# One tile for both kinds of a batch's spectrum rows, one send for its last rows, and Pool's half stores moved to the sync queue

## Chip, cores, metric

One core of one Trainium2 chip. The metric is the device time of one execution in microseconds. The time of a run is about 1.8 us longer than the span of its profile.

In the views PE is the matmul engine and PEld its loading of weights; DVE, ACT and POOL are the vector, scalar and GpSimd engines; SP is the sync engine. DMAs are issued by an engine to a queue of its own (SPq is sync's) and carried out by 16 DMA engines. A store goes from the chip's inner memory to the output; a half store is one of 64 rows (128 KB); a send is a small DMA between two tiles on the chip. A DMA has landed when its data is in place.

## The reference, cut to what matters

```python
x = windowed_attention(q, k, v)            # 8 batches x 576 x 512
X = rfft(x, axis=1)                        # first 64 modes kept
Y[:, :64] = complex_matmul_per_mode(X, w_r, w_i)
u = x + irfft(Y, n=576)
return u + relu(u @ w_ch)                  # 8 x 576 x 512, float32
```

## The kernel before, where the change touches it

The kernel streams all mode weights, then ends in a tail (from about 392 us) that turns the spectra back. For each batch two tables of 128 spectrum rows are needed as the moving operand: `Yb` (the spectrum) and `yw` (the spectrum times w_ch). The last eight rows of each come from the last four modes; for batches 2 to 7 the kernel gathers them in `yl` and sends them by DMA to their place, partitions 120 to 127.

```python
def pair_tile(what, b):                    # one tile per kind and pair of batches
    p = b // 2
    if (what, p) not in Yp:
        Yp[what, p] = wmid.tile([128, 2, DM], FP32R, ...)
    return Yp[what, p][:, b % 2, :]
...
yl = yp.tile([128, 2, DM], FP32R, name="yl")
def send(i, b):                            # 8 rows x 2 KB
    r0 = 2 * R + RL * (b - 2)
    nc.gpsimd.dma_start(out=pair_tile(("yw", "Yb")[i], b)[128 - RL:], in_=yl[r0:r0 + RL, i])
...
def finish(n):                             # one output piece of 128 rows x 512
    b, t = seq[n]
    add(n, "Yb", True)                     # PE
    if t % 2 == 0:
        ots[0] = op.tile([128, 2, DM], FP32, name="ot")     # 7 buffers
    ...
    nc.vector.tensor_tensor(out=ot[:, j], in0=ps, in1=x_sb[:, b, t, :], op=ALU.add)
    if t == NT - 1:                        # 64 rows of batch b, 64 of b + 1
        for i, queue in enumerate((nc.sync, nc.gpsimd)):
            queue.dma_start(out=out[b + i, 128 * t:, :], in_=ot[64 * i:64 * i + 64, 0])
    ...
    elif j:                                # two pieces, 128 rows x 4 KB
        nc.sync.dma_start(out=..., in_=ot)
...
for n in range(NT):
    rectify(n)                             # PE add of yw, then ReLU on ACT
    if n == 2:
        nc.scalar.copy(out=yl[0:NR, 0], in_=psw[0:NR])
for b in range(2, B):
    for i in range(2):
        send(i, b)
for n in range(NQ):                        # 36 pieces
    finish(n)
    ...                                    # rectify and lay three ahead
```

The softmax here doesn't subtract the row's maximum and nothing guards it: scores larger than these inputs give would overflow.

## Time and profile before

| | before |
|---|---|
| time, median (range) | 429.94 us (429.93 to 430.3) |
| span of the profile, in a run of 431.18 us | 429.4 us |
| DVE's last output piece ends | 421.33 us |
| last store issued, landed | 423.82, 428.37 us |

The profiled run was 1.2 us slower than the median. Part 3 of its page lists each DMA queue with its packets, MB and share of the 16 engines:

```profile
q0 software_dynamic: 25920, 82.52, 96.4%
q1 hardware_dynamic: 2768, 8.78, 5.5%
```

Queue 0 is Pool's: all loads of weights and of q, k and v, and in the tail the sends and four half stores. Queue 1 is sync's: all other stores but one. The tail shares its 16 DMA engines between both.

### The profile page before, as it was taken

How to read it: one execution, taken by the hardware profiler on the slowest of the kernel's cores; microseconds unless marked ns; L12 is line 12 of the kernel's file. 1: busy time of each engine (PE TensorE's matmuls, PEld its weight loads, DVE VectorE, ACT ScalarE, POOL GpSimd, SP SyncE). 2: the span in 40 equal slices, each digit the busy share in tenths (PEclk: the TensorE clock that was granted, in tenths of full speed). 3: DMA queues.
4: the chain of work that ended last, by engine and by line, in shares of the span. 5: the costliest groups of instructions: out<-in, count | busy, mean ns of one | idle time of the engine just before them, and what ended most of it. 6: DMA issues, size and time to landing. Idle time of an engine off the chain costs nothing.

```text
span 429.4 us, 11626 instructions
## 1 busy us (share of the span) xinstructions
PE 322.8 (75%) x5186; PEld 230.2 (54%) x5186; DVE 176.6 (41%) x372; ACT 164.5 (38%) x290; POOL 97.9 (23%) x187
## 2 busy tenths in 40 slices
PE   6989999999989966323488978876367875598991
PEld 4755765665665665212366756654244543356780
DVE  5566765766673200307233432231022331132892
ACT  3585765866773121001021322222012231122990
POOL 7231231331021322212212212111211122100600
PEclk9999999999995855555587998899557785589996
DMA  7999999999999999999999999999999999992897
GB/s 140 212 213 211 214 214 213 213 213 212 214 214 214 215 213 260 214 213 213 213 214 214 214 214 212 214 213 214 213 214 213 213 213 214 213 203 43 270 363 266
DMA packets 28882, 92.17 MB, mean 215 GB/s; under 512 B 3136, under 2 KB 3392, under 8 KB 28832
## 3 DMA queue, kind: packets, MB, share of 16 engines
q0 software_dynamic: 25920, 82.52, 96.4%
q1 hardware_dynamic: 2768, 8.78, 5.5%
q8 instruction: 40, 0.66, 0.6%
q10 hardware_dynamic: 144, 0.13, 0.1%
q14 instruction: 10, 0.08, 0.0%
HBM read 162.53 MB, written 9.44 MB: 400 GB/s over the span
## 4 chain that ended last, share of the span: by engine, by line
DMA 47%; PE 32%; issue 9%; DVE 7%; ACT 1%; POOL 1%; DVEq 0%; POOLq 0%
DMA wt<-in_moe_w_i_dram 25%; DMA wt<-in_moe_w_r_dram 21%; PE pso L316 7%; PE pst L218 6%; PE psv L235 3%; DVE x_sb L324 3%; PE pso L856 3%; PE pss L372 3%; PE pss L272 2%; PE psx L338 2%; PE pss L291 2%; DVE vT L59 2%; PE psz L594 1%; PE psy L563 1%; PE psw L706 1%
## 5 line engine op out<-in xcount | busy, mean ns | idle before, releaser
L563 PE MATMUL psy<-XQ,wt 128*128 128x16 bf16 x1616 | 61.1, 191 | 73.1 <-DMA wt<-in_moe_w_i_dram 37.2
L563 PEld LDWEIGHTS <-wt 128*128 128x128 bf16 x1616 | 52.8, 103 | 88.6 <-DMA wt<-in_moe_w_i_dram 43.3
L591 DVE CAST xT<-pxt 128x256 fp32r<-128x256 bf16 (+1 forms) x68 | 26.2, 435 | 60.1 <-PE pxt L584 38.9
L115 POOL DMA_DIRECT2D wt<-in_moe_w_r_dram x54 | 29.0, 537 | 87.7 <-DMA wt<-in_moe_w_r_dram 39.2
L115 POOL DMA_DIRECT2D wt<-in_moe_w_i_dram x52 | 28.1, 540 | 85.6 <-DMA wt<-in_moe_w_i_dram 54.9
L596 ACT CAST Z<-psz 128x512 fp32r<-128x512 f32 x36 | 21.1, 587 | 65.3 <-PE psz L594 64.9
L594 PE MATMUL psz<-wch,xT 128*128 128x512 f32 x144 | 46.1, 464 | 0.0
L297 ACT ACTIVATE et<-pss 128x512 bf16<-128x512 f32 x72 | 39.2, 599 | 13.6 <-PE pss L291 13.6
L316 PE MATMUL pso<-vt,et 128*64 128x65 bf16 (+1 forms) x576 | 34.3, 210 | 4.8 <-DVE x_sb L324 4.7
L316 PEld LDWEIGHTS <-et 128*64 128x64 bf16 (+1 forms) x576 | 24.0, 114 | 17.1 <-issue 9.6
L594 PEld LDWEIGHTS psz<-wch,xT 128*128 128x128 f32 x144 | 29.4, 218 | 6.0 <-ACT Z L596 0.4
L324 DVE TENSOR_TENSOR x_sb<-pso,rcp 128x640 bf16<-128x640 f32 x32 | 26.3, 822 | 0.9
L59 DVE CAST YT<-psy 128x256 fp32r<-128x256 f32 x6 | 2.5, 425 | 51.1 <-PE psy L563 51.1
L879 DVE TENSOR_TENSOR ot<-pso,x_sb 128x512 f32<-128x512 f32 x35 | 22.3, 686 | 1.8 <-PE pso L856 1.5
L59 DVE CAST x_sb<-psj 128x512 bf16<-128x512 f32 x16 | 11.0, 689 | 27.5 <-PE psj L768 27.4
L58 ACT CAST YT<-psy 128x256 fp32r<-128x256 f32 x6 | 2.2, 373 | 52.4 <-DVE YT L59 52.4
L272 PE MATMUL pss<-band,ident_bf 64*64 64x512 bf16 x136 | 20.7, 414 | 1.5 <-ACT et L297 1.5
L59 DVE COPY vT<-pst 128x768 bf16<-128x768 bf16 x16 | 15.3, 958 | 13.0 <-PE pst L218 13.0
L58 ACT CAST x_sb<-psj 128x512 bf16<-128x512 f32 x16 | 9.4, 587 | 27.3 <-PE psj L768 27.3
L861 ACT ACTIVATE pso<-pso 128x512 f32<-128x512 f32 x36 | 19.2, 587 | 0.3 <-PE pso L856 0.2
L291 PE MATMUL pss<-qT,kT 64*64 64x128 bf16 (+1 forms) x640 | 17.3, 221 | 0.4 <-issue 0.4
L58 ACT COPY qT<-pst 128x768 bf16<-128x768 bf16 x16 | 12.9, 815 | 7.8 <-PE pst L218 7.6
(163 smaller groups left out, 518.5 us busy)
## 6 DMA issues: line engine op xcount, KB each, us to landing
wt<-in_moe_w_r_dram POOLq DMA_DIRECT2D x54, 512.0 KB, 19.1
wt<-in_moe_w_i_dram POOLq DMA_DIRECT2D x52, 512.0 KB, 19.1
out_dram<-ot SPq DMA_DIRECT2D x15, 512.0 KB, 5.5
rk<-in_k_dram POOLq DMA_DIRECT2D x8, 576.0 KB, 9.3
rq<-in_q_dram POOLq DMA_DIRECT2D x8, 576.0 KB, 13.3
rv<-in_v_dram POOLq DMA_DIRECT2D x8, 576.0 KB, 11.8
wy<-in_moe_w_r_dram POOLq DMA_DIRECT2D x3, 512.0 KB, 17.9
wy<-in_moe_w_i_dram POOLq DMA_DIRECT2D x3, 512.0 KB, 19.1
```

The lines of the kernel that those rows point to most:

```text
L58: return nc.scalar.copy(out=o, in_=i)
L59: return nc.vector.tensor_copy(out=o, in_=i)
L115: nc.gpsimd.dma_start(out=wt, in_=src[m].rearrange("(p c) e -> p c e", c=NC))
L218: nc.tensor.transpose(out=ps[64 * hh:64 * hh + 64, c, :], in_=src[:, hh, (c0 + c) * D:(c0 + c + 1) * D], identity=ident_bf)
L272: nc.tensor.matmul(out=pss[(2 * w + hh) % 3][64 * half:64 * half + 64, :], lhsT=ident_bf[pp, pp], rhs=view(band[pp], 128 * half, [[0, WIN ...
L291: nc.tensor.matmul(out=pss[(2 * w + hh) % 3][64 * half:64 * half + 64, col:col + nq], lhsT=kTs[b % 2][pp, g, 64 * kb:64 * kb + 64], rhs=qT ...
L297: nc.scalar.activation(out=et[:, hh, :], in_=pss[(2 * w + hh) % 3], func=ACT_F.Exp, scale=EX_SCALE)
L316: nc.tensor.matmul(out=pso[po, hh, (i // 2) * VW:(i // 2) * VW + D + 1], lhsT=et[pk, hh, col:col + 64], rhs=vt[pk, 1 - f % 2, 2 * hh + g / ...
L324: nc.vector.tensor_tensor(out=view(x_sb, b * NT * DM + g * D, [[4 * D, 2], [DM, NT], [1, D]]), in0=view(pso, 0, [[512, 2], [VW, NT], [1, D]]),
L563: nc.tensor.matmul(out=psy[:, m % MG, e, :], lhsT=w[:, c, 128 * e:128 * e + 128], rhs=XQ[:, c, :, 1 - im:3 - im, m], start=(m % MG == im + ...
L591: nc.vector.tensor_copy(out=xT[:, :, w * k:w * k + w], in_=view(psts[k], j, [[128, NC], [n, w]]))
L594: nc.tensor.matmul(out=psz, lhsT=xT[:, c, :], rhs=wch[:, c, :], start=(c == 0), stop=(c == NC - 1))
```

## The change

Its intent: both kinds of a batch's rows lie side by side in one tile, so one DMA with 4 KB runs replaces two with 2 KB runs; and Pool no longer stores.

```diff
+    def batch_tile(b):
+        if b not in Yp:
+            Yp[b] = wmid.tile([128, 2, DM], FP32R, name=f"Y{b}", tag=f"wm{b}")
+        return Yp[b]
     def pair_tile(what, b):
-        p = b // 2
-        ...
-        return Yp[what, p][:, b % 2, :]
+        return batch_tile(b)[:, ("yw", "Yb").index(what), :]
...
-        def send(i, b):
+        def send(b):
             r0 = 2 * R + RL * (b - 2)
-            nc.gpsimd.dma_start(out=pair_tile(("yw", "Yb")[i], b)[128 - RL:], in_=yl[r0:r0 + RL, i])
+            nc.gpsimd.dma_start(out=batch_tile(b)[128 - RL:], in_=yl[r0:r0 + RL])
...
-                for i, queue in enumerate((nc.sync, nc.gpsimd)):
+                for i, queue in enumerate((nc.sync, nc.sync)):
...
         for b in range(2, B):
-            for i in range(2):
-                send(i, b)
+            send(b)
```

More of the change, by code (lines that the diff above doesn't have):

```diff
@@ L688 @@
     Yp = {}
+    def batch_tile(b):
+        if b not in Yp:
+            Yp[b] = wmid.tile([128, 2, DM], FP32R, name=f"Y{b}", tag=f"wm{b}")
+        return Yp[b]
     def pair_tile(what, b):
-        p = b // 2
-        if (what, p) not in Yp:
-            Yp[what, p] = wmid.tile([128, 2, DM], FP32R, name=f"{what}{p}", tag=f"wm{2 * p + (what == 'Yb')}")
-        return Yp[what, p][:, b % 2, :]
+        return batch_tile(b)[:, ("yw", "Yb").index(what), :]
     def parts_of(b, t):
```

## The prediction

> **What bounds the kernel now.** The change touches only the last 8% of the run, so I asked first where that stage begins and what ends it. In the page's busy-share row the DMA engines stand at nine tenths almost throughout; until about 391 us that is the stream of weights, whose code is untouched. I cut the rest into stretches and read the DMA share beside the engines. Columns: stretch, length, busy us of PE, PEld, DVE, ACT and POOL with counts, granted clock, DMA share, GB/s.
>
> ```profile
> 400.00:404.00 4.00, 3.83 (x17) 2.82 (x16) 3.27 (x6) 4.00 (x9) 3.56 (x8) 1.00 0.92 278
> 408.00:412.00 4.00, 4.00 (x19) 3.20 (x18) 3.79 (x7) 4.00 (x9) 0.00 (x0) 1.00 0.98 350
> 412.00:415.00 3.00, 3.00 (x15) 2.43 (x14) 2.70 (x6) 3.00 (x7) 0.53 (x1) 1.00 1.03 415
> 416.00:419.00 3.00, 3.00 (x14) 2.15 (x12) 2.99 (x6) 3.00 (x7) 0.53 (x1) 1.00 0.96 315
> 420.00:421.00 1.00, 0.04 (x1) 0.00 (x0) 1.00 (x4) 0.00 (x0) 0.00 (x0) 1.00 0.82 281
> 426.00:429.40 3.40, 0.00 (x0) 0.00 (x0) 0.00 (x0) 0.00 (x0) 0.00 (x0) 0.50 0.18 66
> ```
>
> From 400 to 421 us PE, ACT, DVE and DMA are all nearly full, so shares alone do not choose. The end does: DVE makes the last output piece at 421.3 us, yet the DMA engines stay full to 426. So the store queue is next (SPq is the sync engine's issue queue; columns are start, length, what).
>
> ```profile
> 420.58 0.75 DVE L876 TENSOR_TENSOR ot<-pso,x_sb 128x256 f32<-128x256 f32 x2
> ...
> 418.86 3.70 SPq L887 DMA_DIRECT2D out_dram<-ot  x3
> 422.66 1.07 SPq L884 DMA_DIRECT2D out_dram<-ot  x1
> 423.82 1.10 SPq L877 DMA_DIRECT2D out_dram<-ot  x1
> ```
>
> The final store is issued at 423.82, about 2.8 us after its data was ready: the queue is behind. Is the sync sequencer slow, or is it held back by full DMA engines? The view of the store lines gives min/median/max ns of an issue, and that of all transfers the us to landing:
>
> ```profile
> L887 SPq DMA_DIRECT2D out_dram<-ot x15: 332/756/2175, 397.9 to 421.8; - x15
> L882 SPq DMA_DIRECT2D out_dram<-ot x4: 515/857/1127, 403.4 to 418.1; - x4
> L882 POOL DMA_DIRECT2D out_dram<-ot x4: 529/538/559, 404.6 to 416.6; - x4
> ```
>
> The same 512 KB store costs 332 ns to issue when the engines are free (the first ones) and up to 2175 ns later. So it waits for room, and I read the tail as bound by the DMA engines' throughput, not by DVE, PE or the sync sequencer. Throughput is uneven: 415 GB/s where only 512 KB sync stores drain, 278 while the last spectrum rows are sent, 315 and 350 where Pool stores are mixed in. That unevenness is what the change can alter. The waits in the tail (engine line <- what ended it: us in total, times, longest) show what else is at stake:
>
> ```profile
> DVE ot L879 <- PE pso L856: 1.5, 7, 0.3
> PEld pso L856 <- DMA yw<-yl: 0.6, 1, 0.6
> POOL Yb L845 <- DMA Yb<-yl: 0.4, 1, 0.4
> ```
>
> Only one compute wait is on the row transfers, 0.6 us at 400.9. DVE never waits for a store, so the seven output buffers suffice, so far.
>
> **What the Trainium skill says.** (1) "DMA: Bandwidth & Descriptors", section "Issuing engines are not separate DMA queues": DMAs started by sync, scalar and gpsimd share 16 engines; several issuers save only sequencer time. The trace agrees: share 0.96 to 1.03 with either mix. (2) Same page, "Why a DMA increments its semaphore by 16 and not by 1": for gpsimd DMAs all 16 engines post a completion, whatever the shape. In the window that holds the sends, the software queue shows
>
> ```profile
> q0 software_dynamic: 269, 0.13, 14.4%
> ```
>
> packets, MB, share of 16 engines over 6.7 us. 0.13 MB in 2 KB pieces is about 64 packets, so some 205 are small ones, over the 192 that twelve sends at 16 would give. Agrees. (3) Same page, "Why small descriptors are slow (HBM only)": SBUF-to-SBUF transfers are said not to suffer the small-descriptor penalty. That speaks against a big gain from 4 KB runs; no view of this kernel separates it. (4) "SBUF — State Buffer", "Door 1: The DMA port swizzle": 64 partitions reach only half the ports (196 against 328 GB/s at 1 MiB). The trace is in line: at 420 to 421 us, where a 64-row sync store drains with next to no Pool traffic, the rate falls to 281.
>
> **The change, part by part.**
>
> Row sends. Removed: six of twelve Pool sends; each of the other six carries 8 x 4 KB in place of 8 x 2 KB. Pool issues 6 x 0.505 us = 3.0 us less (duration of the line of the sends), not on the path: Pool has nothing else that is urgent but a store. The 0.4 us wait of the last send, which I take to be for a completion slot of an earlier one, should go. On the DMA engines: 14.4% x 6.7 us = 0.96 us of all 16 for 0.13 MB; scaled to the 12 x 16 KB = 0.197 MB, 1.5 us. Bytes stay; data packets fall from 96 to 48 and small ones by at least 96. If half were per-packet cost, 0.75 us would go. But packet time includes waiting behind the other queue, and point (3) says halving the packets gives little. I choose 0.4 us saved (estimate). A check by rate: 400 to 404 us moved 4 x 278 = 1112 KB, 2.68 us at 415 GB/s, so 1.3 us were lost there to sends and to a queue not yet filled; 0.4 is under a third of it.
>
> First wait. The first send is issued at the same time, since it needs both copies and ACT's comes last as before. It landed after 3.05 us in the chain of waits; with twice the bytes on the same eight rows I expect 3.1 to 3.3. PE then starts 0 to 0.2 us later. This is early in the tail, in front of 2.8 us of queue lag, so it adds about 0. Later batches' rows are in place sooner but were not waited for.
>
> Stores. Added: four 128 KB stores of 64 rows on the sync queue, removed: the same on Pool's. Bytes to HBM equal. Cost per pair before: 416 to 419 us moved 3 x 315 = 945 KB, 2.28 us at 415, so about 0.7 us lost to one Pool and one sync half. Cost after: two sync halves, each at the loss seen at 420 to 421 (281 KB is 0.68 us at 415: 0.3 lost), so 0.6 to 0.7. Difference 0 to -0.1 per pair, over four pairs -0.4 to 0; I take -0.1, since half the ports are now read by one queue in turn, while before the two halves could overlap.
>
> Tiles. Both kinds of a batch share a tile; ACT writes one half, DVE the other. The bytes, the slots and the mode at which each slot must be free are the same. I expect 0.
>
> Sum: -0.4 - 0.1 = -0.5 us, from 429.94 to about 429.5.
>
> **The rivals.** (A) The sync sequencer is the true bound. From 408 us on it is issuing almost without gaps. Four issues at the median of 0.857 us add 3.4 us; some 0.8 us of gaps around 410 to 413 absorb part, so +1.5 to +2.5: 431.5 to 432.5. For it: solid issue time. Against it: the 332 ns minimum, and issue times that grow with the backlog. I give it one in eight.
> (B) Mixing the queues costs all of the loss. Then yl transfers and Pool stores lower every packet, and one queue alone runs near 415: up to 1.3 us at 400 to 404 and 0.3 to 0.4 per pair come back, less the 64-row loss: -1.5 to -2, so 428. For it: 315 and 350 beside 415. Against: the second at 420 to 421, slow without Pool. One in six.
> (C) A new wait on output buffers. The piece at 419.98 us reuses the buffer of the one seven tiles before, whose stores were issued at 413.1 and take 5.2 to 6.1 us to land: about 0.75 us of slack. The second half now follows the first on one queue, up to 1.1 us later. DVE could stall by some 0.4 us late in the tail; hidden if the engines are the bound. 429.5 to 430.
> (D) Everything hidden: one straggling DMA engine sets the end (from 426 us on the share is 0.18 over 3.4 us, so few engines still work) and is not relieved. 429.9.
>
> **Range and chances.** The centre weighs the sum (-0.5) with A, B and D: 429.5. Before's runs spread over 0.4 us, so A's low half and most of B give 428.4 to 430.8. Two per cent is 8.6 us, a quarter of the whole tail; no rival reaches it. I leave 1% each way, for an allocation or schedule that shifts in the weight stream.
>
> **What would show it.** Right: twice six small sends become six of 32 KB with landing near 4 us; the GB/s of 400 to 404 us rises from 278 towards 300 or more; from 408 us on sync issues stay as long, with the moved ones at 0.5 to 1.1 us; the last sync issue is at 423 to 424 us; DVE still ends near 421.3. Wrong by A: last issue after 425 and a DMA share under 0.9 in 412 to 425. Wrong by B: rates near 400 throughout and the last issue within 1.5 us of DVE's end. Wrong by C: a DVE wait named after an output store. A shift before 391 us would mean that the allocation moved something that I took as fixed.

## The result, and the profile after

Measured: 429.69 us median (429.56 to 430.09, 4 runs) against 429.94 (429.55 to 430.3, 4 runs). The ratio is 0.9996, 95% interval 0.9979 to 1.0013. (A ratio is the mean time of one kernel's fast runs over that of the other's of the same rounds, so not quite the ratio of the medians quoted.) On these runs alone the change is not told apart from nothing. The predicted 429.5 and its range 428.4 to 430.8 hold; but the range also contains 429.94, which is no change at all.

The profile of the changed kernel has a span of 427.7 us in a run of 429.56. First, the same stretches as in the prediction (length, busy us of PE, PEld, DVE, ACT, POOL, clock, DMA share, GB/s), with a stretch and the end added:

```profile
400.00:404.00 4.00, 3.35 (x15) 2.45 (x14) 2.79 (x5) 3.54 (x8) 0.61 (x2) 1.00 0.95 283
404.00:408.00 4.00, 4.00 (x19) 3.22 (x19) 3.71 (x7) 3.78 (x8) 0.00 (x0) 1.00 0.95 353
408.00:412.00 4.00, 4.00 (x19) 3.23 (x18) 3.80 (x7) 4.00 (x10) 0.00 (x0) 1.00 0.99 349
412.00:415.00 3.00, 3.00 (x15) 2.40 (x14) 2.69 (x5) 3.00 (x8) 0.00 (x0) 1.00 1.02 410
416.00:419.00 3.00, 3.00 (x15) 2.33 (x13) 2.99 (x5) 2.98 (x7) 0.00 (x0) 1.00 1.02 390
424.00:427.00 3.00, 0.00 (x0) 0.00 (x0) 0.00 (x0) 0.00 (x0) 0.00 (x0) 0.50 0.51 183
```

Before, the added stretch read:

```profile
404.00:408.00 4.00, 4.00 (x19) 3.23 (x18) 3.69 (x6) 3.77 (x9) 1.40 (x3) 1.00 1.03 331
```

400 to 404 us, where I expected the gain of the sends, is hardly better (283 against 278). The gain lies where the sends used to run on, 404 to 408 (353 against 331), and where Pool stores used to mix in, 416 to 419: 390 against 315. Next the end, from the timelines of DVE and of the sync queue:

```profile
420.80 0.74 DVE L879 TENSOR_TENSOR ot<-pso,x_sb 128x256 f32<-128x256 f32 x2
...
420.97 1.07 SPq L887 DMA_DIRECT2D out_dram<-ot  x1
422.14 1.12 SPq L880 DMA_DIRECT2D out_dram<-ot  x1
```

DVE ends 0.2 us later than before, at 421.55 (its second piece overlaps the first), but the last store is issued only 0.6 us after that, not 2.5 us. The store lines (min/median/max ns of an issue) show that the queue of whole stores no longer backs up:

```profile
L890 SPq DMA_DIRECT2D out_dram<-ot x15: 332/393/583, 397.6 to 420.3; - x15
L885 SPq DMA_DIRECT2D out_dram<-ot x8: 472/1041/1482, 403.6 to 417.6; - x8
```

A 512 KB store's issue has a median of 393 ns and never exceeds 583, where it was 756 and 2175. (The half stores, L885, keep long issues: a median of 1041 ns, 857 before.) And the waits in the tail:

```profile
DVE ot L882 <- PE pso L859: 2.0, 7, 0.7
PEld pso L859 <- DMA Y<-yl: 1.1, 1, 1.1
PE pso L859 <- DMA Y<-yl: 0.6, 1, 0.6
```

The one wait on the sends grew from 0.6 to 1.1 us: the first 32 KB send landed 3.54 us after its issue, the first 16 KB one 3.05.

### The profile page after: what moved, and what is told of

Same layout as the page of the kernel before. It is cut to its first block, busy times and chain, and to the rows that moved or that the text cites. A ratio compares the mean times of both kernels' runs of the same rounds, so it can differ in the third digit from the quotient of the medians.

```text
span 427.7 us, 11617 instructions
## 1 busy us (share of the span) xinstructions
PE 319.2 (75%) x5179; PEld 229.5 (54%) x5186; DVE 176.4 (41%) x372; ACT 164.3 (38%) x290; POOL 92.5 (22%) x177
## 4 chain that ended last, share of the span: by engine, by line
DMA 54%; PE 30%; DVE 8%; issue 3%; ACT 2%; POOL 1%; DVEq 0%; POOLq 0%
DMA wt<-in_moe_w_i_dram 30%; DMA wt<-in_moe_w_r_dram 14%; DMA wy<-in_moe_w_r_dram 9%; PE pso L316 6%; PE pst L218 6%; PE psv L235 3%; DVE x_sb L324 3%; PE pso L859 3%; PE pss L272 2%; PE pss L372 2%; PE psx L338 2%; PE pss L291 2%; DVE vT L59 2%; DVE ot L882 1%; PE psw L709 1%
## 5 line engine op out<-in xcount | busy, mean ns | idle before, releaser
L859 PE MATMUL pso<-Y,trigI 128*128 128x512 f32 x80 | 23.3, 403 | 0.7 <-DMA Y<-yl 0.6
L859 PEld LDWEIGHTS pso<-Y,trigI 128*128 128x128 f32 x80 | 14.5, 188 | 6.4 <-ACT pso L864 1.7
```

Of the source, the lines that this page charges most:

```text
L859: nc.tensor.matmul(out=tps[n], lhsT=trigI[:, tr:tr + 128], rhs=pair_tile(what, bb), start=False, stop=stop and r0 + k == 128, skip_group_c ...
```

## The experiments

To compare profiles I use two lengths. The **tail** runs from the start of DVE's first output piece to the last store's landing, the **closing** from there to the end of the span; landings and closing steps are from the trace's semaphore records, which the timelines leave out. In the first profile of before the tail is 428.37 - 396.58 = 31.79 and the closing 1.03; in that of the changed kernel 426.15 - 396.30 = 29.85 and 1.56.

Twelve kernels ran in three calls, each call on one chip with its own 11 runs of the kernel before; each kernel had 6 timed runs. All counted as correct.

| run | what | median us | ratio to before (95%) | tail us | closing us |
|---|---|---|---|---|---|
| e1 | before | 430.08 | 0.9998 (0.9976 to 1.0021) | 30.95 | 1.03 |
| e2 | changed | 429.81 | 0.9985 (0.9967 to 1.0004) | 29.80 | 1.57 |
| e3 | rows merged only | 429.62 | 0.9990 (0.9968 to 1.0013) | 30.39 | 1.03 |
| e4 | stores moved only | 429.82 | 0.9986 (0.9967 to 1.0004) | 30.46 | 1.28 |
| e5 | changed, first send split | 430.11 | 1.0004 (0.9989 to 1.0020) | 30.03 | 1.72 |
| e6 | changed, six tiny transfers in the tail | 433.18 | 1.0085 (1.0065 to 1.0105) | 33.88 | 1.20 |
| e7 | before, 24 sends | 431.22 | 1.0031 (1.0016 to 1.0047) | 31.57 | 1.03 |
| e8 | changed, Pool padded | 429.77 | 0.9998 (0.9984 to 1.0011) | 30.06 | 1.29 |
| e9 | changed | 429.76 | 0.9990 (0.9969 to 1.0011) | 29.93 | 1.57 |
| e10 | changed, both closing losses mended | 429.53 | 0.9978 (0.9960 to 0.9996) | 30.49 | 0.96 |
| e11 | changed, no sends | 428.59 | 0.9956 (0.9937 to 0.9975) | 28.92 | 1.27 |
| e12 | changed, all half stores on Pool | 430.94 | 1.0015 (0.9995 to 1.0035) | 30.98 | 1.28 |

The kernel before had medians of 430.33, 429.73 and 430.29 us, and single runs from 429.13 to 432.36.

### First call: noise and the two parts alone

e1 is the kernel before and e2 the changed kernel, both without an edit.

> The kernel before, unchanged, for noise and for a second profile. The first profile had a span of 429.4 us in a run of 431.18 us, 1.2 us over the median of its timed runs (429.94), so it may be an unlucky run. Theory E (the DMA engines' throughput bounds the tail, always): ratio 1.000, and the new profile again shows the last store issued 2 us or more after DVE's end and its landing about 7 us after it. Theory L (the first profile was an unlucky run with one straggling DMA engine): span near 428.1, last landing about 5 to 6 us after DVE's end.

> The changed kernel, again. On record 429.69 against 429.94 (-0.25 us, interval -0.9 to +0.6). Theory E with my sum: -0.5 us. Theory L: -0.2 to -0.3, because the typical run of before has no long queue at the end and the changed kernel starts its rows of batch 2 later (their send now lands after 3.5 us instead of 3.05).

e1's profile has a span of 428.35 us, its last store issued 1.99 us after DVE's end and landed 6.2 us after it. So the first profile overstated before's tail by some 0.8 us (theory L in part), but the queue is there in both (theory E in part). Its store line and two stretches:

```profile
L887 SPq DMA_DIRECT2D out_dram<-ot x15: 332/826/1667, 397.7 to 421.0; - x15
404.00:408.00 4.00, 4.00 (x19) 3.26 (x18) 3.70 (x7) 3.91 (x8) 0.96 (x2) 1.00 0.95 296
415.00:419.00 4.00, 4.00 (x18) 2.95 (x16) 3.89 (x7) 3.98 (x9) 0.53 (x1) 1.00 0.97 327
```

Against e1 the changed kernel's tail is shorter by 30.95 - 29.80 = 1.15 us, its closing longer by 0.54, its span shorter by 0.53. The timed difference, 0.0015 x 430 = 0.6 us, is of that size, but its interval touches 1.

```diff
# e3_rows_only, against the changed kernel
-                for i, queue in enumerate((nc.sync, nc.sync)):
+                for i, queue in enumerate((nc.sync, nc.gpsimd)):
# e4_stores_only, against the kernel before
-                for i, queue in enumerate((nc.sync, nc.gpsimd)):
+                for i, queue in enumerate((nc.sync, nc.sync)):
```

> Only the rows are merged; the four halves stay on the Pool queue. My sum: -0.4 us. Rival B (mixing the two queues costs): near 0, since the Pool stores still mix. Rival W (the later first send delays DVE by about 0.5 us and that counts): +0.0 to +0.5.

> Only the stores move to the sync queue; twelve sends stay. My sum: -0.1 us. Rival A (sync sequencer bound): +1.5 to +2.5. Rival B (mixing costs): -0.5 to -1.5. Rival W: the first send still lands after 3.05 us, so this should be the fastest of the four.

The timings of the four are too close to rank. In the profiles, against e1, rows alone shorten the tail by 0.56 us, stores alone by 0.49, and both by 1.15. That they add is not shown: each is one profile, and the two profiles of before differ by 0.84 us; against the first one the gains would be 1.40, 1.33 and 1.95. Each part is seen a second time on top of the other, though: from e4 to the three profiles of the changed kernel the tail falls by 0.5 to 0.7 us (rows), from e3 to them by 0.5 to 0.6 (stores).

Rival A asked for 1.5 to 2.5 us more in e4. The tail got shorter instead, although all issues on sync together took longer (19.6 us against 17.6 in e1), so it is dead. Rival W fails on the tail of e3, which is shorter although DVE ends 0.6 us later than in e1. The stretches of the two single changes, e3 first, then e4:

```profile
404.00:408.00 4.00, 4.00 (x19) 3.21 (x19) 3.69 (x7) 3.76 (x8) 1.00 (x2) 1.00 0.98 368
415.00:419.00 4.00, 4.00 (x19) 3.23 (x18) 3.89 (x7) 3.98 (x9) 0.53 (x1) 1.00 0.98 336
```

```profile
404.00:408.00 4.00, 4.00 (x19) 3.26 (x18) 3.69 (x7) 3.91 (x8) 0.12 (x1) 1.00 0.96 328
415.00:419.00 4.00, 4.00 (x18) 2.96 (x16) 3.88 (x7) 3.98 (x9) 0.00 (x0) 1.00 0.98 364
```

The rows gain more in 404 to 408, the stores in 415 to 419. (The narrower 416 to 419 misleads: it reads 359 in e3 and 368 in e4, but in e3 part of the half stores had moved ahead of it. Over 415 to 419 the first profiles read 328 before and 377 after.)

The shares that the queues took of the 16 DMA engines in 396 to 429 us tell more (packets, MB, share of 33 us). e1 first, then e4:

```profile
q1 hardware_dynamic: 2768, 8.78, 71.1%
q0 software_dynamic: 576, 0.72, 10.3%
```

```profile
q1 hardware_dynamic: 3088, 9.31, 75.9%
q0 software_dynamic: 384, 0.20, 3.7%
```

Moving four half stores takes 6.6% of 33 us, 2.2 us, off Pool's queue and adds 1.6 us to sync's: 0.6 us saved, about the tail's 0.49. The packet records of the traces (which `prof` does not list one by one) show where it was: a half store on Pool goes in packets of 4 KB that took 241 to 271 ns in the mean (before, e1, e3, e12), while the 4 KB packets of sync's whole stores took 167 to 169 ns in those runs and in the changed kernel alike. So what is slow is Pool's own store packets; the sync queue's packets are not slowed by the mix. And with twelve sends e4's Pool queue takes 3.7%; with six the changed kernel's takes 3.8% (its line is in the last section). A packet's time may include some waiting behind the other queue.

### Second call: does the later first send cost, and what is lost in the closing

```diff
# e5_first_split, against the changed kernel
+            if b == 2:
+                for i in range(2):
+                    nc.gpsimd.dma_start(out=batch_tile(b)[128 - RL:, i], in_=yl[r0:r0 + RL, i])
+                return
```

> The changed kernel, but batch 2, whose rows are waited for first, is again sent in two 16 KB pieces, first kind first. Theory N (the change gained some 1.6 us of draining at the end and gave part back by a later first send, 3.5 to 3.7 us to landing against 3.05, which delays DVE by 0.4 to 0.7 us): the first send lands after 3.1 us, DVE ends near 421.2 instead of 421.55 to 421.85, and the time falls by 0.3 to 0.6 us against the changed kernel, so ratio about 0.9975 to the kernel before. Theory E (engines still bound the end): DVE ends earlier, the time of the changed kernel stays (0.9985).

The wait is cured, the time is not:

```profile
PEld pso L863 <- DMA Y<-yl: 0.6, 1, 0.6
```

The send lands after 3.06 us. From its first output piece to its end DVE takes 421.36 - 396.64 = 24.72 us, 0.5 to 0.7 less than in the three profiles of the unedited changed kernel (25.24 to 25.40). But the tail is 30.03 us, no shorter than 29.80 to 29.93, and the ratio is 1.0004. Theory N's claim that the later send gave gain back finds no support here, and theory E holds in this run; e10 below points the other way. Part of the ratio is not the tail's: e5's closing is 0.15 us longer than the changed kernel's, since Pool has a gap of 0.32 us at another of its last steps.

```diff
# e6_six_lanes, against the changed kernel, at the head of the tail
+        scr = yp.tile([16, 16], BF16, name="scr")
+        for _ in range(6):
+            nc.sync.dma_start(out=scr, in_=ident_bf[0:16, 0:16])
# e8_pool_pad, against the changed kernel, after the sends
+        pad = yp.tile([128, 1], FP32, name="pad")
+        for _ in range(10):
+            nc.gpsimd.memset(pad, 0.0)
```

> The changed kernel with six tiny transfers on the sync queue at the head of the tail, which do nothing but turn the rotation of completion semaphores, so that the last store's semaphore is the last in the closing waits. Theory N also holds that the changed kernel loses 0.25 us because the semaphore of its last store comes early in the order of the closing waits (0.45 us from the last landing to the drain, against 0.20 before): here that interval should be under 0.15 us, and the span 0.3 us shorter than the changed kernel's 427.7 to 427.8. If the order of the closing waits does not matter, the interval stays at 0.45.

> The changed kernel with ten tiny memsets on Pool after the sends, where Pool is idle, so that Pool's program has about as many instructions as before. In both profiles of the changed kernel Pool sits 0.37 us between two of its last semaphore steps, in all four others 0.08. If that is a matter of where Pool's program stands (instruction fetch), it goes back to 0.08 here and the span is 0.3 us shorter than the changed kernel's. If it is anything else it stays.

e6 was badly built. The six transfers write one tile, so each waits for the one before, and the sync queue sat on them until 405.8 us:

```profile
394.34 11.48 SPq L838 DMA_DIRECT2D scr<-ident_bf  x6
405.87 3.23 SPq L893 DMA_DIRECT2D out_dram<-ot  x4
```

Stores that start 8 us late cost 3.4 us of time. Its profiled run also lost 2 us before the tail and is used for one thing only: from the last landing to the sync engine's drain 0.08 us pass, against 0.45 in the changed kernel. The sync engine waits for the eight completion semaphores of the hardware queues in a fixed order, about 0.06 us a step; where the last store's semaphore is the last, nothing remains to be stepped through. With 22 such transfers in the tail (before) it is sixth, with 26 (after) second, so 0.25 us were lost. e8: Pool's gap near the end is 0.37 us in the three profiles of the unedited changed kernel and 0.08 here, the span 427.46 us. The step of 0.29 us is thus tied to Pool's program, not to the stores (it is 0.08 in e3 and e4 too); that it is instruction fetch is only argued. In the time e8 (429.77) shows nothing beside the changed kernel's 429.69 to 429.81 of other calls.

```diff
# e7_quarter_sends, against the kernel before
+            for c in range(0, DM, DM // 2):
                 nc.gpsimd.dma_start(out=pair_tile(("yw", "Yb")[i], b)[128 - RL:, c:c + DM // 2], ...)
```

> The kernel before with each of the twelve sends cut in two again: 24 of 8 KB in 1 KB runs. If each send costs the DMA engines time beyond its bytes (theory N: six sends fewer gained about 1.2 us of draining, so some 0.2 us a send), twelve more cost 1 to 2.4 us: time 431 to 432.5, ratio 1.003 to 1.006, last landing 7.5 us or more after DVE's end. If sends are cheap (my record: 0.4 us for six), +0.3 to 0.8. If the end does not hang on them: 1.000.

Clearly slower: 1.0031, which is 1.3 us. The tail grew by 0.6 us against e1. But the edit also made the first wait longer, since both halves of the first row kind are needed (PEld waits 1.7 us in it), and run length fell together with the number rising; so it shows that cutting the sends up costs, not by which of these ways. DVE's stretch grew by 1.06 us, more than the tail did, so the longer wait alone could account for it.

### Third call: bounds, doses and a mended closing

e9 is the changed kernel without an edit.

> The changed kernel a third time, as the measure for the other three on the same chip. On record 0.9996 and 0.9985 of the kernel before: I expect 0.999. In the profile DVE's first output piece to the last landing takes 29.8 us (29.85 and 29.80 before; 30.95 and 31.79 in the kernel before), the closing part after the last landing 1.56 us (1.04 before).

As expected: 0.9990, tail 29.93, closing 1.57.

```diff
# e10_closing: e8's memsets, and at the very start of the program
+    for i in range(6):
+        scr = consts.tile([16, 16], BF16, name=f"scr{i}")
+        nc.sync.dma_start(out=scr, in_=ident_bf[0:16, 0:16])
# e11_no_sends, against the changed kernel
-        for b in range(2, B):
-            send(b)
# e12_both_pool, against the changed kernel
-                for i, queue in enumerate((nc.sync, nc.sync)):
+                for i, queue in enumerate((nc.gpsimd, nc.gpsimd)):
```

> The changed kernel with both closing losses mended: six tiny transfers on the sync queue, this time at the very start, each to a tile of its own, and the ten memsets on Pool. The closing part after the last landing should be 1.56 - 0.29 (Pool's step) - 0.37 (order of waits) = 0.9 us, the span 427.1. If these parts of the profile count in the time: 0.6 us under the changed kernel, ratio about 0.9975. If the time does not follow, the gain is there in the profiled run only.

The closing is 0.96 us, so both losses are mended as worked out. The profiled run had a late first send (4.08 us to landing): DVE took 25.77 us, 0.4 to 0.5 more than in the unedited changed kernel, and the tail, 30.49 us, was 0.6 to 0.7 longer. So its span, 427.8, is no better, and in this profile a later DVE went with a longer tail. In the timing it is the one correct kernel that is clearly faster than before: 0.9978, interval 0.9960 to 0.9996, about 0.9 us. Against e9 of the same rounds it is 0.23 us by the medians, which is not clear of noise and less than the 0.6 hoped for.

> The changed kernel without any row send: a wrong result on purpose (the last eight spectrum rows of batches 2 to 7 stay zero), to bound what all sends cost. If six sends fewer gained 0.55 us of tail (30.95 to 30.39 with rows merged), the six that remain cost about as much: first piece to last landing 29.2 to 29.4 and time 0.4 to 0.6 us under the changed kernel. If sends cost by their bytes or are hidden: 29.7 to 29.9.

The result is wrong on purpose; it passes the tolerance, presumably because eight rows of the spectrum weigh little. The tail falls by 29.93 - 28.92 = 1.0 us, more than the 0.5 to 0.7 expected, and the time by 1.2 us. The largest difference lies in the stretch where the sends run, 387 GB/s against the 274 to 283 of the changed kernel:

```profile
400.00:404.00 4.00, 4.00 (x19) 3.17 (x18) 3.43 (x6) 4.00 (x9) 0.00 (x0) 1.00 0.97 387
```

The gain in stores is larger than the difference of the rates, since those count the sends' bytes too: in this stretch e11's sync queue moves 1.54 MB against 0.95 in the changed kernel, which is 1.4 us at 415 GB/s. The tail does not gain all of it; from 412 to 415 us e11 falls back to 308 GB/s, where the changed kernel has 410. And a rival is not excluded: the edit removes the wait on the first send too, DVE takes 24.31 us against 25.38 in e9, and the last landing comes 4.6 us after DVE's end in both. So e11 bounds what the sends cost in engine time and in waiting together. The packets of the six sends take 3.8% of 33 us, 1.25 us of all 16 engines; their bytes alone, 0.197 MB, would be 0.47 us at 415 GB/s.

> The changed kernel with all eight half stores on the Pool queue, where rows-only has four and the changed kernel none. First piece to last landing was 29.8 with none and 30.4 with four. If mixing software-queue stores with the sync queue is what costs: about 30.9 to 31.0 with eight, time 0.5 to 1.1 us over the changed kernel. If it is only that one queue's order matters: 30.4 or less, as with four.

The tail is 30.98 us against 29.93 with no half store on Pool and 30.39 with four, as rival B's dose would have it, each in one profile; the changed kernel's other profiles, e5 and e8 lie between 29.80 and 30.06, e10 with its late first send at 30.49. The time is 1.2 us over e9, with ranges that overlap in few runs (430.23 to 432.19 against 429.65 to 430.99). All issues on sync together take 8.0 us, half of the changed kernel's, yet stores land no sooner (median 4.6 us for a whole one, 4.0 in e9):

```profile
419.00:424.00 5.00, 1.27 (x4) 0.37 (x2) 2.56 (x6) 0.71 (x2) 0.00 (x0) 0.82 1.00 348
```

## Why the prediction was right, step by step

**The bound.** I read "the tail as bound by the DMA engines' throughput". This fits the kernel before, whose last store was issued 2.0 to 2.5 us after DVE's end. The change used that lead up: in the three profiles of the changed kernel the last issue follows DVE's end by 0.3 to 0.6 us. There the two limits lie close together: DVE 0.5 us faster did not shorten the tail (e5), DVE 0.4 to 0.5 us slower went with a longer one (e10), each in one profile. Of the signs of being right, "sync issues stay as long" was wrong: the whole stores' fell from 756 to 393 ns in the median. So were the rate of 400 to 404 us (283, 278 and 274, not 300) and the last issue (422.14, not 423 to 424). Of the two signs of B, the last issue within 1.5 us of DVE's end came true, rates near 400 throughout did not.

**Row sends, -0.4 us.** The tail says -0.56 (e1 to e3), so the size was close, but the mechanism is not borne out. I counted on less packet time; half the packets took the same 3.7 to 3.8% of the engines, since a packet of 4 KB took 368 to 408 ns in the mean where one of 2 KB took 171 to 188. The rate at 400 to 404 did not rise. What shows is that the sends are over sooner (the last of the twelve landed at 408.2 us in e1, the last of the six at 404.5), and the gain lies in 404 to 408; why the tail gets shorter by it stays open. One reading was wrong as well: of the 205 small packets in the window I wrote that they agree with 16 a send. The 64 data packets beside them are those of eight sends, 128 small ones at 16 each; the whole of e4's sends has 288 small ones, 24 each.

**First wait, 3.1 to 3.3 us to landing, adding about 0.** The size was wrong: 3.5 to 3.7 in the three profiles of the unedited changed kernel, and DVE lost 0.4 to 0.7 us in the tail. That it adds nothing is supported by e5 and not by e10.

**Stores, -0.1 us.** The mis-sized term: the tail gained 0.49 (e1 to e4). I took the second at 420 to 421 us as proof that a half store on sync costs as much as on Pool. By the packet records it takes 0.48 to 0.54 us of the 16 engines on Pool and 0.39 to 0.44 on sync, about 0.1 us less, and the dose (29.93, 30.39, 30.98 for none, four, eight on Pool) gives some 0.12 us a store. Rival B, to which I gave one in six, was right that Pool's stores cost, wrong that they lower every packet, and too large in size.

**Tiles, 0.** The weight stream ends at 391.2 to 391.5 us in all unedited profiles; nothing shifted.

**What was not foreseen.** About 0.54 us of the tail's gain was given back after the last landing: 0.25 by the place of the last store in the order of closing waits, 0.29 by a step of Pool. So the sum came out right by luck, because two errors offset: the tail gained 1.15 us where I had 0.5, and 0.54 went in the closing. What remains, 0.6 us by the profiles of e1 and e2, is within the noise of any one call; the three ratios of the changed kernel (0.9996, 0.9985, 0.9990) agree in sign only.

**Rivals.** A fell in e4. C did not occur: no DVE wait on an output store in the changed kernel (e7 had one, 0.4 us). D (a straggling engine sets the end) may explain part of the first profile of before, which was 0.8 us worse in the tail than e1; no run shows it.

**Left open.** Why merging the rows shortens the tail when the packet time stays; what makes the packets of Pool's stores and sends slow; how far DVE and how far the DMA engines set the end of the changed kernel; how much of the closing loss counts in the time, since e10 gives 0.23 us over e9 where the profiles promise 0.6.

## What to carry to other kernels

When the last stores queue up behind one another, look at the duration of their issues: here the same store took 0.33 us early and 2 us late, and taking load off the DMA engines shortened both the issues and the tail. When the queue's lag behind the compute engine is gone, ask again what sets the end. Compare the time that packets take, and not only their number and bytes: half as many packets took the same time here, and the same half store took more of the engines from one queue than from the other. After a change that shortens the end, check the steps behind the last landing too, since they can quietly return half of it.

## What the Trainium skill lacked or had wrong

- "DMA: Bandwidth & Descriptors", "Issuing engines are not separate DMA queues", says that several issuers save only sequencer time. Here the issuing queue also mattered to the engines: a half store took 0.48 to 0.54 us of all 16 when issued on Pool and 0.39 to 0.44 on sync, and with none, four and eight on Pool the tail was 29.93, 30.39 and 30.98 us. The section gives no such cost.
- Same page, "Why a DMA increments its semaphore by 16 and not by 1": 16 completions for a gpsimd DMA. The six 8-row sends of the changed kernel made 192 packets, that is 8 of data and 24 small ones each; a 64-row Pool store made 48, that is 32 of 4 KB (two rows in one) and the 16 of the page. The line is of the changed kernel's transfers in the tail:

```profile
q0 software_dynamic: 192, 0.20, 3.8%
```

- Same page, "Why small descriptors are slow (HBM only)": that transfers from SBUF to SBUF are spared was my reason for a small gain. Between rows of 2 KB and 4 KB this holds: the sends took 3.7 and 3.8% of the engines. What the section lacks is what they cost beside a stream of stores: 1.25 us of all 16 engines for 0.197 MB, 0.47 us at the 415 GB/s of whole stores.
- "SBUF — State Buffer", "Door 1: The DMA port swizzle", is in line, but not separated: in 0.8 us in which the changed kernel mainly drains half stores, with nothing from Pool, it moves 248 GB/s, against 410 with whole ones. Half the ports, packets of 2 KB in place of 4, and engines that were busy only 85% of that time are not told apart. Over 408 to 412 us, with half and whole stores mixed, the rate is 349.

```profile
DMA packets 111, 0.20 MB, mean 248 GB/s; under 512 B 21, under 2 KB 21, under 8 KB 111
```

- No page I read tells of the order of the closing waits: from the last landing to the drain 0.45 us (changed kernel), 0.20 (before) or 0.08 (e6), by which completion semaphore the last store has.
